# A decode block on one core: gate and up products moved behind the first scores, the down weights' load moved behind the fourth K tile

## The chip, the core and the metric

The kernel runs on one core of one Trainium2 chip. The metric is the device time of one execution in microseconds (us), the median of several runs. Its engines appear in the profile as PE (TensorE, matrix products; PEld is its weight load), DVE (VectorE), ACT (ScalarE), POOL (GpSimd) and SP (SyncE, which here only issues loads and the store of one output row). 16 DMA engines move the data; "SPq" is SP's issue queue.

## What is computed

One decode step for two sequences: attention over a cache of 32,768 keys with 32 query heads on 8 key/value heads, times the SiLU of a gated MLP, plus the input. All is float32.

```python
x = A_x                                   # [2, 1, 512]
xn = layernorm(x)
q = xn @ wq                               # 32 heads of 128
scores = q . k_cache * 128 ** -0.5        # k_cache [2, 8, 32768, 128]
s = (softmax(scores) @ v_cache) @ wo      # wo [4096, 512]
gate, up = xn @ W_gate, xn @ W_up         # [512, 1792] each
g = silu(((gate * (gate > 0)) * up) @ W_down)   # W_down [1792, 512]
return x + s * g
```

K and V caches together are 537 MB, which have to come from memory once; all weights are 28 MB.

## The kernel before

The work goes in 64 tiles. A tile is 8,192 keys of one sequence and one key/value head: four tiles make a group (one sequence, one head), 16 groups make all. A K tile is one load of 4 MB, [128 partitions, 4 chunks, 16 rows, 128]. V comes mostly in double tiles of 8 MB.

The loop of lines 524 to 567 runs over stages `s`. In stage `s`, DVE transposes K tile `s` in four parts (`k_transpose`, line 290, tile `kts`), with other DVE steps between the parts; PE makes the scores of tile `s` (`scores`, line 302, 32 matmuls); DVE copies the scores of tile `s - 1` out of PSUM (`take_scores`, line 316). Four stages later, after the softmax of the group (`tile_maximum`, `maximum`), come the tile's weights (`weights`, `take_weights`), and in odd stages the products of two tiles with V (`values`, line 374).

The small MLP is fitted into the first stages: `mlp_gu` makes the gate and the up product (32 matmuls each, line 242), `mlp_take` copies each out of PSUM (line 253), `mlp_h` gates them and transposes the result (lines 258 to 263), and `mlp_down` makes the down product (28 matmuls, line 277), whose SiLU is taken on ACT. The dictionaries `extra`, `taken` and `ahead` say in which stage such a step is called: `taken` right after `take_scores`, `extra` after the stage's scores and values, and `ahead` at the end of the stage, for loads.

What sets the order:

- PE and DVE run their instructions in the order of the calls: `pin` chains them, stage by stage. A step that waits holds all that is called later on its engine.
- All big loads go out through `load` (line 128) on SP's queue, in the order of the calls. SP waits in order too: a load whose buffer isn't free holds all loads behind it.
- The pool `ring` has two slots, tag "r". K tiles use them in turn, so K tile t + 2 can be loaded when the transposes of K tile t are done.
- The pool `wide` has one slot, tag "w". It holds one after the other `wq` (query weights), `wgu` (gate and up weights, two loads), `wd` (down weights), and then the double V tiles. Each of these loads waits until the last reader of the one before is done: `wd` for the up product, the first V tile for the down product.

The loads are called in this order before: wq, K0, K1, the two of wgu (before the loop); K2 (stage 0); wd, K3 (stage 1); K4 (stage 2); K5 and the first double V tile (stage 3); K6 (stage 4), and so on. In the text, K0 is the first K tile, K3 the fourth.

On PE the products of the MLP are called in this order: scores(0), scores(1), gate, up, scores(2), down, scores(3). `mlp_take` and `mlp_h` are called in stage 2, after `take_scores(1)`, and so stand on DVE between the first and the second part of K2's transposes.

Of the kernel before, what the change touches and what calls it, by code (L numbers as in the profile page):

```python
# [24 lines left out]
def kernel(  # L25
# [449 lines left out]
    extra, taken, ahead = {}, {}, {}  # L475

    def at(where, s, f, *a):
        where.setdefault(s, []).append((f, a))

    END = NK + NU  # L480
    at(ahead, 1, load_d)
    for s in range(NK - 2):
        at(ahead, s, load_k, s + 2)
        if s % 2 and s >= 3:
            at(ahead, s, load_vv, s - 3)
    at(ahead, NK - 2, load_v, NK - 4)
# [1 line left out]
    at(ahead, NK - 1, load_vv, NK - 2)  # L488
    at(ahead, NK + 1, load_wo, 0, 4)
    at(ahead, NK + 1, load_wo, 4, HKV)  # L490
    at(extra, 1, mlp_gu, "g")
    at(extra, 1, mlp_gu, "u")
    at(taken, 2, mlp_take, "g")
    at(taken, 2, mlp_take, "u")
    at(taken, 2, mlp_h)
# [107 lines left out]
```

## Time and profile before

| | us |
|---|---|
| median of 3 runs | 1330.86 |
| lowest, highest | 1330.72, 1330.94 |
| the profiled execution | 1330.93 |
| its span, first to last instruction | 1329.1 |

| engine | busy us | share of the span |
|---|---|---|
| PE (matmuls) | 908.2 | 68% |
| DVE | 707.1 | 53% |
| ACT | 52.1 | 4% |
| DMA queue of SP | | 98.6% of 16 engines |

How to read the lines that follow. A row of a timeline has the start in us, the duration in us, the engine, the line of the kernel, the operation, what it writes and reads with its shapes, and how many instructions were merged into the row; in brackets stands how long the engine was idle before and what ended that. A row of SP's issues (DMA_DIRECT2D) shows when a load was issued, not when it landed; merged rows reach from the first issue to the end of the last. A row of the waits has the waiting engine and line, what released it, the total in us, how often, and the longest. A row of a cut by time has the stretch, its length, the busy time and number of instructions of PE, PEld, DVE, ACT and POOL, then the clock granted to PE as a share of full speed, the mean busy share of the DMA engines, and the GB/s that they moved. The releaser of a wait is inferred by the profiler.

### The profile page before, as it was taken

Reading aid. Unit: us, or ns where it says so; the run is one execution under the profiler, and the core shown is the slowest. Engines: PE = TensorE matmul, PEld = TensorE weight load, DVE = VectorE, ACT = ScalarE, POOL = GpSimd, SP = SyncE. Lnnn points to the kernel's source line nnn. Section 1 sums busy time; section 2 is a strip of 40 time slices with the busy share of each in tenths; the row PEclk is TensorE's granted clock in tenths of the full one; section 3 lists DMA queues with packets and bytes.
Section 4 is the critical chain, followed back from the end, with each engine's and each line's share of the span. In section 5 each row is a group of like instructions: output and inputs, shape, how many; then the busy total and the mean of one; then the engine's idle time right before and its main releaser. Section 6 shows DMA issues by size and latency. Waiting matters only on the chain.

```text
span 1329.1 us, 10685 instructions
## 1 busy us (share of the span) xinstructions
PE 908.2 (68%) x4736; PEld 216.8 (16%) x4736; DVE 707.1 (53%) x667; ACT 52.1 (4%) x136; POOL 0.7 (0%) x6
## 2 busy tenths in 40 slices
PE   3586667776775776767568676757767676776775
PEld 1121111121111111111111111112111111111112
DVE  3848445466644546656454665545466554546610
ACT  0001000000000000000000000000000000000000
POOL 0000000000000000000000000000000000000000
PEclk9799788878878887878897778888889777987887
DMA  9979999999999999999999999999999999999997
GB/s 411 427 314 411 440 415 423 440 427 439 436 438 427 432 427 436 431 442 438 426 428 431 435 432 438 432 440 424 430 432 437 439 428 438 430 427 431 444 429 307
DMA packets 16962, 565.36 MB, mean 425 GB/s; under 512 B 1794, under 2 KB 1810, under 8 KB 3988
## 3 DMA queue, kind: packets, MB, share of 16 engines
q1 hardware_dynamic: 16888, 564.67, 98.6%
q8 instruction: 37, 0.61, 0.2%
q14 instruction: 9, 0.07, 0.0%
q10 hardware_dynamic: 28, 0.01, 0.0%
HBM read 564.67 MB, written 0.00 MB: 425 GB/s over the span
## 4 chain that ended last, share of the span: by engine, by line
DMA 66%; DVE 26%; PE 7%; issue 1%; DVEq 0%
DMA k<-in_A_k_cache_dram 60%; DVE kts L290 21%; DMA v<-in_A_v_cache_dram 5%; PE s L302 2%; PE o_ps L374 2%; DMA wq<-in_A_wq_dram 2%; DVE sc L316 1%; DVE os L396 1%; DVE ob L416 1%; PE pr L344 1%; PE pq L201 1%; DVE qt L220 0%; PE po L426 0%; PE py_near L446 0%; PE py L465 0%
## 5 line engine op out<-in xcount | busy, mean ns | idle before, releaser
L290 DVE STREAM_TRANSPOSE kts<-k 128x2048 f32<-128x2048 f32 x256 | 578.0, 2287 | 462.8 <-DMA k<-in_A_k_cache_dram 462.8
L302 PE MATMUL s<-kts,qt 128*32 128x512 f32 x2048 | 490.0, 729 | 186.6 <-DVE kts L290 183.3
L374 PE MATMUL o_ps<-v,sc 128*16 128x512 f32 x2048 | 258.7, 646 | 80.3 <-DMA v<-in_A_v_cache_dram 80.3
L302 PEld LDWEIGHTS s<-kts,qt 128*32 128x32 f32 x2048 | 97.0, 128 | 579.0 <-DVE kts L290 322.2
L374 PEld LDWEIGHTS o_ps<-v,sc 128*16 128x16 f32 x2048 | 62.4, 102 | 255.8 <-issue 167.1
L352 ACT ACTIVATE sc<-sc,nb 128x512 f32<-128x512 f32 x64 | 45.4, 710 | 1130.4 <-DVE nb L348 1130.4
L358 PE MATMUL pt<-sc,perm 128*128 128x512 f32 x128 | 85.4, 757 | 1.3 <-ACT sc L352 1.3
L316 DVE TENSOR_SCALAR_CACHE_REDUCE sc<-s 128x512 f32<-128x512 f32 x64 | 43.1, 673 | 58.9 <-PE s L302 58.9
L330 PE MATMUL pr<-ident,m 128*1 128x128 f32 x16 | 5.2, 327 | 79.3 <-DVE m L328 79.3
L367 DVE STREAM_TRANSPOSE sc<-pt 128x512 f32<-128x512 f32 x64 | 43.3, 676 | 12.7 <-PE pt L358 12.4
L344 PE MATMUL pr<-negone,mrow 1*128 1x1 f32 x32 | 8.9, 344 | 33.4 <-DVE mrow L341 33.4
L358 PEld LDWEIGHTS pt<-sc,perm 128*128 128x128 f32 x128 | 22.0, 215 | 54.1 <-issue 39.2
L413 PE MATMUL po<-os,head 128*4 128x512 f32 x32 | 28.2, 982 | 0.0
L394 DVE RECIPROCAL rl<-pl 128x1 f32<-128x1 f32 x16 | 2.6, 164 | 26.4 <-PE pl L389 26.4
L330 PEld LDWEIGHTS pr<-ident,m 128*1 128x1 f32 x16 | 1.3, 79 | 94.0 <-DVE m L328 92.1
L396 DVE SCALAR_TENSOR_TENSOR os<-o_ps,rl,own 128x512 f32<-128x512 f32 x16 | 12.0, 751 | 8.3 <-PE o_ps L374 6.8
L344 PEld LDWEIGHTS pr<-negone,mrow 1*128 1x128 f32 x32 | 7.5, 290 | 37.4 <-DVE mrow L341 37.4
L201 PE MATMUL pq<-wq,xt 128*32 128x512 f32 x64 | 8.8, 715 | 6.7 <-DMA wq<-in_A_wq_dram 6.7
L416 DVE TENSOR_REDUCE ob<-po 4x128 f32<-4x512 f32 x16 | 10.6, 662 | 4.5 <-PE po L413 4.3
L277 PE MATMUL ps_d<-wd,ht 128*32 128x512 f32 x28 | 12.2, 592 | 0.0
L352 ACT ACTIVATION_READ_ACCUMULATOR sc<-sc,nb 128x1 f32 x64 | 11.9, 186 | 0.0
L426 PE MATMUL po<-ident,ob 64*64 64x4 f32 x64 | 4.6, 244 | 10.5 <-DVE ob L416 10.5
(74 smaller groups left out, 107.6 us busy)
## 6 DMA issues: line engine op xcount, KB each, us to landing
k<-in_A_k_cache_dram SPq DMA_DIRECT2D x64, 4096.0 KB, 26.7
v<-in_A_v_cache_dram SPq DMA_DIRECT2D x2, 4096.0 KB, 29.5
wo<-in_A_wo_dram SPq DMA_DIRECT2D x7, 1024.0 KB, 17.7
wgu<-in_B_W_gate_dram SPq DMA_DIRECT2D x1, 3584.0 KB, 19.9
wgu<-in_B_W_up_dram SPq DMA_DIRECT2D x1, 3584.0 KB
wd<-in_B_W_down_dram SPq DMA_DIRECT2D x1, 3584.0 KB
wo<-in_A_wo_dram SPq DMA_DIRECT2D x1, 512.0 KB
wo<-in_A_wo_dram SPq DMA_DIRECT2D x2, 256.0 KB
```

The source lines that it names most:

```text
L201: nc.tensor.matmul(pq[half][32 * c : 32 * c + 32, :], xn[:, k, :], wqt[:, k, half, c * 512 : (c + 1) * 512], start=(k == 0), stop=(k == NK ...
L290: nc.vector.transpose(part.rearrange("p r e k -> p (r e k)"), KT[t][:, c].rearrange("p r d -> p (r d)"))
L302: nc.tensor.matmul(ps[Q * c : Q * c + Q, :], qt[:, b, hk, e, :], kts[c][:, :, e, :], start=(e == 0), stop=(e == 3),)
L316: nc.vector.tensor_scalar(ST[t].rearrange("p r m -> p (r m)"), SPS.pop(t), SCALE, None, op0=ALU.mult, op1=ALU.max, accum_out=MX[g][:, u : ...
L344: nc.tensor.matmul(pr[:, 256:257], mrow.rearrange("o c k h -> o (c k h)"), negone, start=True, stop=True)
L352: nc.scalar.activation(st, st, AF.Exp, bias=nbias, scale=1.0, accum_out=LS[g][:, u : u + 1])
L358: nc.tensor.matmul(PW[t], perm.rearrange("p k c h -> p (k c h)"), ST[t].rearrange("p r m -> p (r m)"), start=True, stop=True,)
L367: nc.vector.transpose(ST[t].rearrange("p r m -> p (r m)"), PW.pop(t))
L374: nc.tensor.matmul(ops[g % 2][a : a + NC * REP, :, :], w[:, r, : NC * REP], v[:, :, r, :], start=(u == 0 and r < 4), stop=(u == NU - 1 and ...
L396: nc.vector.scalar_tensor_tensor(OS[g], ops[g % 2], rl, own.unsqueeze(2).to_broadcast([P, NC, DH]), op0=ALU.mult, op1=ALU.mult,)
L413: nc.tensor.matmul(po[mine, :], head, o.rearrange("p c d -> p (c d)"), start=True, stop=True)
L416: nc.vector.reduce_sum(ob[mine, :], po[mine, :].rearrange("p (c d) -> p d c", c=NC), axis=AX.X)
```

## The change

The gate and up products are called in stage 0, behind scores(0), and no longer in stage 1, behind scores(1). The load of `wd` is called in stage 1 behind that of K3, and no longer ahead of it. The copies out of PSUM, the gating and the down product stay in stage 2, at their places. No instruction is added or taken away.

```diff
     END = NK + NU
-    at(ahead, 1, load_d)
     for s in range(NK - 2):
         at(ahead, s, load_k, s + 2)
+        if s == 1:
+            at(ahead, s, load_d)
         if s % 2 and s >= 3:
             at(ahead, s, load_vv, s - 3)
...
-    at(extra, 1, mlp_gu, "g")
-    at(extra, 1, mlp_gu, "u")
+    at(extra, 0, mlp_gu, "g")
+    at(extra, 0, mlp_gu, "u")
     at(taken, 2, mlp_take, "g")
     at(taken, 2, mlp_take, "u")
     at(taken, 2, mlp_h)
     at(extra, 2, mlp_down)
```

So the calls of the loads become wq, K0, K1, wgu, K2, K3, wd, K4, K5, first V tile, K6; and on PE scores(0), gate, up, scores(1), scores(2), down, scores(3).

## The prediction

> **What bounds the kernel now.** I read the page first: its busy shares, the DMA row over time, and the chain that ended last.
>
> ```profile
> span 1329.1 us, 10685 instructions
> DMA  9979999999999999999999999999999999999997
> GB/s 411 427 314 411 440 415 423 440 427 439 436 438 427 432 427 436 431 442 438 426 428 431 435 432 438 432 440 424 430 432 437 439 428 438 430 427 431 444 429 307
> DMA 66%; DVE 26%; PE 7%; issue 1%; DVEq 0%
> ```
>
> No engine is full, but the DMA engines are busy in nine tenths or more of nearly every slice, and two thirds of the chain is waiting for DMA. So the kernel lives on one stream of loads out of SP's queue. The exception is the third slice: 7 tenths and 314 GB/s. I cut that region by time, beside the long stretch after it.
>
> ```profile
> core 0: us, PE busy (x) PEld busy (x) DVE busy (x) ACT busy (x) POOL busy (x), PEclk, DMA share, GB/s
> 66.00:78.00 12.00, 9.79 (x92) 4.21 (x84) 5.63 (x8) 0.00 (x0) 0.00 (x0) 0.95 0.26 89
> 104.00:110.00 6.00, 4.58 (x28) 0.95 (x28) 4.60 (x3) 0.00 (x0) 0.00 (x0) 1.00 0.69 257
> 148.00:1300.00 1152.00, 800.20 (x4061) 185.07 (x4059) 621.72 (x540) 43.94 (x120) 0.00 (x0) 0.83 1.00 433
> 66.00:148.50 82.50, 60.06 (x319) 15.30 (x311) 43.28 (x36) 5.28 (x13) 0.00 (x0) 0.91 0.87 369
> 67.50:68.00 0.50, 0.50 (x12) 0.19 (x8) 0.00 (x0) 0.00 (x0) 0.00 (x0) 1.00 0.16 66
> 76.50:77.00 0.50, 0.00 (x0) 0.00 (x0) 0.48 (x1) 0.00 (x0) 0.00 (x0) 1.00 2.22 573
> ```
>
> The last column is GB/s. From 148 to 1300 us the stream moves 433 GB/s. From 66 to 78 us it moves 89 x 12 = 1.07 MB, which at 433 takes 2.5 us, so 9.5 us are lost: it all but stops before 67.5 us, I say at 67.3, and resumes between 76.5 and 77.0, I say at 76.7. From 104 to 110 us it moves 1.54 MB, worth 3.6 us: another 2.4 us lost. Together 11.9 us. The row from 66 to 148.5 checks it: 82.5 us at 369 GB/s is 30.4 MB, which at 433 is 70.3 us, so 12.2 us lost. I take 12.0.
>
> Who stops the stream? SP's own queue tells, its issues first, then what it waited for.
>
> ```profile
> 51.23 0.33 SPq L128 DMA_DIRECT2D k<-in_A_k_cache_dram  x1
> 75.82 0.33 SPq L128 DMA_DIRECT2D wd<-in_B_W_down_dram  x1
> 76.25 9.30 SPq L128 DMA_DIRECT2D k<-in_A_k_cache_dram  x2
> 106.08 0.33 SPq L128 DMA_DIRECT2D k<-in_A_k_cache_dram  x1
> 118.25 11.41 SPq L128 DMA_DIRECT2D k<-in_A_k_cache_dram  x2
> ...
> SPq L128 <- PE ps_u L242: 15.8, 1, 15.8
> SPq L128 <- DMA wgu<-in_B_W_up_dram: 8.4, 1, 8.4
> SPq L128 <- DVE sb_u L253: 0.2, 1, 0.2
> ```
>
> The issue at 51.23 is the third K tile (K2), the last thing in the stream when it dries up. Behind it in the queue stands wd (the down weights). It needs the one "w" buffer, which holds wgu until the gate and up products have read it: SP waits 8.4 us for the up weights to land (so they are there by 51.56 + 8.4 = 60.0 us), then 15.8 us for the last up product, and issues at 75.82. K3 stands behind wd and goes at 76.25. Was K3 held only by the queue? Its slot is K1's, which DVE gives free:
>
> ```profile
> 48.89 4.51 DVE L290 STREAM_TRANSPOSE kts<-k 128x2048 f32<-128x2048 f32 x2
> 58.37 6.69 DVE L290 STREAM_TRANSPOSE kts<-k 128x2048 f32<-128x2048 f32 x3
> 69.65 2.31 DVE L290 STREAM_TRANSPOSE kts<-k 128x2048 f32<-128x2048 f32 x1 [4.59 <-DMA k<-in_A_k_cache_dram]
> 71.88 0.65 DVE L316 TENSOR_SCALAR_CACHE_REDUCE sc<-s 128x512 f32<-128x512 f32 x1
> 75.83 0.62 DVE L253 COPY sb_u<-ps_u 128x448 f32<-128x448 f32 x1 [2.38 <-PE ps_u L242]
> 78.54 6.66 DVE L290 STREAM_TRANSPOSE kts<-k 128x2048 f32<-128x2048 f32 x3
> 96.54 2.31 DVE L290 STREAM_TRANSPOSE kts<-k 128x2048 f32<-128x2048 f32 x1 [11.34 <-DMA k<-in_A_k_cache_dram]
> 148.49 2.31 DVE L290 STREAM_TRANSPOSE kts<-k 128x2048 f32<-128x2048 f32 x1 [18.58 <-DMA k<-in_A_k_cache_dram]
> ```
>
> K1's four transposes end at 58.37 + 6.69 = 65.1 us. The same reading fits the other K issues: K2 goes at 51.23, when K0's last transpose is through, and the second issue in the 76.25 row (K4, 76.25 + 9.30 - 0.33 = 85.2) when K2's is, 78.54 + 6.66 = 85.2. So K3 was ready 11 us before it was issued, with 2 us of stream still ahead of it.
>
> **The change part by part.** No instruction and no byte is added or removed. Two things move.
>
> *wd behind K3 on SP.* K3's issue now follows K2's, and goes when K1's transposes are done: 65.1 us. From an issue to its first bytes is about 1.0 us (75.82 to the 76.5-77.0 window). The stream needs it by 67.3 - 1.0 = 66.3, so the gap closes with 1.2 us to spare. wd now waits in SP's queue with K4 behind it, and needs the gate and up products done.
>
> *The products behind scores(0).* The PE rows:
>
> ```profile
> 51.25 6.46 PE L302 MATMUL s<-kts,qt 128*32 128x512 f32 x28 [3.07 <-DVE kts L290]
> 65.11 4.23 PE L302 MATMUL s<-kts,qt 128*32 128x512 f32 x25 [0.28 <-DVE kts L290]
> 68.76 0.92 PE L242 MATMUL ps_g<-wgu,xt 128*32 128x448 f32 x6
> 75.25 0.54 PE L242 MATMUL ps_u<-wgu,xt 128*32 128x448 f32 x1
> 88.29 11.75 PE L277 MATMUL ps_d<-wd,ht 128*32 128x512 f32 x27
> 106.11 3.62 PE L302 MATMUL s<-kts,qt 128*32 128x512 f32 x26 [1.15 <-DVE kts L290]
> ```
>
> scores(0) ends at 57.7; PE then has little to do until K1's last transpose at 65.1. The 64 products took from 68.76 to 75.79, 7.0 us. Moved into that hole they run from 57.7 to 64.7 (the up half starts at 61.2, after its weights' 60.0). So wd can go at 65.5, right behind K3; the stream wants it by 76.0. scores(1) is not delayed: it still starts in earnest at 65.1. If the cover is gone (the products start only at 60.0 and run at half rate, 14 us), they end at 74.0, scores(1) waits behind them on PE, and DVE's take_scores(1) behind that; the price is worked out under the rivals.
>
> *What is late next.* I followed the queue with the stream as the clock: K tiles are 4,096 KB (4.19 MB, 9.7 us at 433), wd 3,584 KB (8.5 us), a double V tile twice a K tile, 19.4 us:
>
> ```profile
> k<-in_A_k_cache_dram SPq DMA_DIRECT2D x64, 4096.0 KB, 26.7
> wd<-in_B_W_down_dram SPq DMA_DIRECT2D x1, 3584.0 KB
> ```
>
> K2's bytes end at 67.3, K3's at 77.0, wd's at 85.5, K4's at 95.2, K5's at 104.9. Each issue is due 1.0 us before.
> - K4, due 84.5: K2 still lands at 69.65. After it DVE runs as before, but no longer waits for the up product: take_scores(1) at 71.88, the two product copies from 72.5, the second at about 73.1. From that copy to the end of K2's transposes was 85.20 - 75.83 = 9.4 us, so K4 goes at 82.5. Two us to spare.
> - K5, due 94.2: K3 is there, so DVE runs stage 3 straight on: one transpose to 84.7; scores(2) from 82.5 for 3.6 us (the 106.11 row) to 86.1; the copy 0.6; three transposes 6.7: 93.4. With scores(2) wholly at the slow rate (6.5 us, the 51.25 row) it is 96.3, and 2.1 us are lost. The row of the same work with PE freshly busy (65.11) has 4.2 us, and gives 94.0, in time. I take 0.3 us, between 0 and 2.1.
> - The first V tile, due 103.9: it needs the down product. wd's bytes end at 85.5 and land some 2.3 us later (K2: 67.3 to 69.65), so 87.8, about where the down product started before; it takes 12 us and ends at 99.9. In time. scores(3) now queues behind it on PE until 103.5, which delays DVE's stage 4, but K6 is due only at 104.9 + 19.4 - 1.0 = 123.3 and went 8.5 us after scores(3) (118.25 less 106.11 + 3.62), so 112 now. Cover: 11 us.
> - So the second gap (104 to 110), which came from K5 (106.08) waiting for K3's late transposes (the first at 96.54), also closes.
>
> From K6's landing on, everything waits for the stream: DVE stood idle 18.58 us before the 148.49 row. scores(3), with which its stage 4 starts, ends only 6 us earlier (103.5 against 106.11 + 3.62 = 109.7) while K6 lands 12 earlier, so some 12 us of this wait remain and nothing else becomes the bound. From there each landing simply moves up, to the tail. In the tail one thing hangs on when PE wakes:
>
> ```profile
> 1305.21 5.83 PE L374 MATMUL o_ps<-v,sc 128*16 128x512 f32 x32 [12.16 <-DMA v<-in_A_v_cache_dram]
> 1311.28 3.63 PE L374 MATMUL o_ps<-v,sc 128*16 128x512 f32 x32
> ```
>
> The same 32 products took 5.83 us after an idle stretch and 3.63 when running. Waking at another moment may cost up to 1.6 us more (all slow: 6.46 us for 28 at 51.25 makes 7.4 for 32) or 2.2 less; I take no difference.
>
> Sum: -12.0 + 0.3 = -11.7 us. The profiled execution took 1330.93 us, 1.8 beyond its span, and 0.07 more than the median of the runs shown; on the median, 1330.86 - 11.7 = 1319.2 us.
>
> **The rivals.** *K3 is held by something else* (the change doesn't do what it says). One row speaks for it: the 0.2 us wait that ends at 76.25 is put to the second product copy. If that is K3's true release, the copy's new time, 73.1, sets K3: bytes at 74.1 instead of 76.7, 2.6 us gained, and the second gap's 2.4, so 1325.9. Against it: that copy ends at 75.83 + 0.62 = 76.45, after the issue, and K2, K4 and K5 all went with a transpose. Chance 0.05.
>
> *PE is late.* Products ending at 74.0 as above. From their end to K4: scores(1)'s remainder 3.6, its copy 0.7, then 0.6 and 9.4 from the copies to the last transpose, 14.3 us. K4 at 88.3 against 84.5 loses 3.8: 12.0 - 3.8 = 8.2, so 1322.7. Against it: the clock column reads 0.50 at 56.5 and 1.00 at 57.0, just before the products start, and PE then stays busy.
>
> ```profile
> 56.50:57.00 0.50, 0.50 (x6) 0.06 (x2) 0.00 (x0) 0.00 (x0) 0.00 (x0) 0.50 0.40 172
> 57.00:57.50 0.50, 0.50 (x4) 0.00 (x0) 0.00 (x0) 0.00 (x0) 0.00 (x0) 1.00 1.73 745
> 60.50:61.00 0.50, 0.27 (x1) 0.18 (x2) 0.50 (x2) 0.00 (x0) 0.00 (x0) 0.50 1.97 852
> ```
>
> For it: the clock had fallen again at 60.5 after a 3 us pause. Chance 0.06.
>
> *Slower.* The same place, K4 behind wd behind the products, but with the products held on PE by their weights. Loss starts when they end after 84.5 - 14.3 = 70.2, eats the gain at 82.2 and passes 0.2% (2.7 us, about what a measurement can tell from no change) at 84.9: 1333.6 us and more. That needs the up weights to land 18 us later than 60.0 (84.9 less 7.0 is 77.9), and nothing ahead of them in the queue moves. Chance 0.03.
>
> *No change.* The stream, unbroken here, goes no faster than the 369 GB/s it averages with its gaps; then the gaps were no loss: 1330.9 us. Against it stands the 433 of the following 1152 us, with the same kinds of loads. [...] Chance 0.03.
>
> **How the numbers follow.** The forecast has 0.83. Its own range runs from -12.0 - 2.2 (nothing lost at K5, the tail all fast: 1316.7) to -12.0 + 2.1 + 1.6 (both at their worst: 1322.6). Both bounds of the tail at full length are unlikely, since it woke from idleness before and will again, so the low end is 1317.5; the high end reaches to PE being late, 1322.7. K3 held (0.05), no change and slower (0.03 each) stay outside. Faster by over 0.2%: 0.83 + 0.05 + 0.06 = 0.94; within 0.03; slower 0.03.
>
> **What would show it.** In the changed profile SP issues K3 at about 65 us and wd within 1 us of it; the windows from 66 to 78 and from 104 to 110 us read about 430 GB/s; the gate and up products run between 57.7 and 65; K4 goes near 82.5 and K5 near 93.5; DVE's wait before K6 ends at about 136.5 instead of 148.49, and lasts some 12 us instead of 18.6; from there the busy times per stage are as before. I am wrong if K3's issue comes with a copy rather than with a transpose, if a new hole opens ahead of K4, K5 or the first V tile, or if the 12 us gained at K6 are no longer there at the last V tile (1305.2 before, 1293 expected).

## The result, and the profile after

The changed kernel takes 1320.32 us (median of 5 runs, 1319.49 to 1322.04), the kernel before 1330.94 (5 runs): 10.6 us less, a ratio of 0.9922 (95% interval 0.9908 to 0.9935). The forecast was 1319.2, the range 1317.5 to 1322.7. The profiled execution is one of the longer ones: 1321.72 us, with a span of 1319.9, 9.2 less than the span before. Of the runs below, one execution (the first run of the early copies) took 1801.64 us, which nothing here explains; it is left out of that run's median and ratio.

The page of the changed kernel: span, DMA by slices, GB/s by slices.

```profile
span 1319.9 us, 10685 instructions
DMA  9999999999999999999999999999999999999997
GB/s 408 433 412 427 433 441 437 424 430 434 431 435 445 428 429 429 435 429 437 435 443 422 427 436 435 435 441 425 428 429 437 437 436 431 433 427 431 436 431 295
```

The third slice now reads 9 and 412; no slice but the last is below 408. Then the stream by stretches (last column GB/s, the clock granted to PE two columns before it):

```profile
66.00:78.00 12.00, 3.93 (x24) 0.63 (x13) 8.25 (x10) 0.00 (x0) 0.00 (x0) 0.78 1.00 429
78.00:84.00 6.00, 5.37 (x12) 0.76 (x16) 6.00 (x4) 0.00 (x0) 0.00 (x0) 0.50 0.96 416
90.00:96.00 6.00, 6.00 (x15) 1.54 (x14) 5.35 (x3) 0.00 (x0) 0.00 (x0) 1.00 0.90 388
96.00:104.00 8.00, 7.70 (x42) 1.94 (x40) 2.52 (x2) 2.35 (x5) 0.00 (x0) 1.00 0.95 373
104.00:110.00 6.00, 1.91 (x5) 1.08 (x5) 5.26 (x8) 1.93 (x5) 0.00 (x0) 0.74 1.20 519
148.00:1300.00 1152.00, 791.20 (x4086) 183.59 (x4085) 612.45 (x535) 43.93 (x120) 0.00 (x0) 0.83 1.00 433
```

66 to 78 us went from 89 to 429 GB/s, 104 to 110 from 257 to 519: both holes are gone. A shallow one has come in between: 388 and 373 from 90 to 104. SP's issues and the DVE rows show where:

```profile
52.31 12.98 SPq L128 DMA_DIRECT2D k<-in_A_k_cache_dram  x2
65.47 0.33 SPq L128 DMA_DIRECT2D wd<-in_B_W_down_dram  x1
82.42 13.28 SPq L128 DMA_DIRECT2D k<-in_A_k_cache_dram  x2
100.30 0.33 SPq L128 DMA_DIRECT2D v<-in_A_v_cache_dram  x1
...
69.68 2.31 DVE L290 STREAM_TRANSPOSE kts<-k 128x2048 f32<-128x2048 f32 x1 [4.74 <-DMA k<-in_A_k_cache_dram]
73.04 0.61 DVE L253 COPY sb_u<-ps_u 128x448 f32<-128x448 f32 x1
88.04 0.69 DVE L316 TENSOR_SCALAR_CACHE_REDUCE sc<-s 128x512 f32<-128x512 f32 x1 [3.45 <-PE s L302]
138.89 2.31 DVE L290 STREAM_TRANSPOSE kts<-k 128x2048 f32<-128x2048 f32 x1 [14.26 <-DMA k<-in_A_k_cache_dram]
```

K3 goes at 52.31 + 12.98 - 0.33 = 64.96 us (76.25 before), right when K1's transposes are done, wd at 65.47, K4 at 82.42, K5 at 82.42 + 13.28 - 0.33 = 95.37 (106.08 before), the first V tile at 100.30. K6 is there at 138.89 where it was at 148.49: 9.6 us of the 12.0 have arrived. Behind that the two executions are alike: the last V tile's products start at 1295.46 against 1305.21, 9.75 earlier, and the span is 9.2 shorter.

PE and its clock:

```profile
57.32 2.90 PE L242 MATMUL ps_g<-wgu,xt 128*32 128x448 f32 x25
60.36 2.87 PE L242 MATMUL ps_u<-wgu,xt 128*32 128x448 f32 x28
64.99 3.62 PE L302 MATMUL s<-kts,qt 128*32 128x512 f32 x26 [0.96 <-DVE kts L290]
80.26 1.91 PE L302 MATMUL s<-kts,qt 128*32 128x512 f32 x2 [0.28 <-DVE kts L290]
82.45 5.55 PE L302 MATMUL s<-kts,qt 128*32 128x512 f32 x26 [0.28 <-DVE kts L290]
88.09 11.75 PE L277 MATMUL ps_d<-wd,ht 128*32 128x512 f32 x27
...
85.50:86.00 0.50, 0.50 (x8) 0.13 (x4) 0.00 (x0) 0.00 (x0) 0.00 (x0) 0.50 0.61 262
86.50:87.00 0.50, 0.50 (x9) 0.13 (x2) 0.00 (x0) 0.00 (x0) 0.00 (x0) 1.00 0.15 66
```

The products stand in the hole behind scores(0) and are through before 64; scores(1) is on time. But scores(2) takes 5.55 us where 3.62 was counted: the clock column is at 0.50 until 86 us. Before the change the products ran up to 75.8; now PE has almost nothing to do from 68.6 to 78 (1.33 us of matmuls in 9.4). The clock falls at 72.73 and rises at 86.38: here it stayed at 0.50 through the two pairs of matmuls from 78 on, 1.91 us in every 2.2, and through the first 3.9 us of scores(2).

In other executions it rose earlier. Two experiments below run the same instructions up to scores(2), but for one that clears an added tile, and add work only later; in the profile of one of them (useless work in stage 9) the clock rises as the second pair ends, and scores(2) takes 3.62 us:

```profile
82.00:82.50 0.50, 0.46 (x1) 0.00 (x0) 0.50 (x1) 0.00 (x0) 0.00 (x0) 0.50 0.53 229
82.50:83.00 0.50, 0.26 (x4) 0.16 (x8) 0.50 (x2) 0.00 (x0) 0.00 (x0) 0.89 1.33 573
82.74 3.62 PE L310 MATMUL s<-kts,qt 128*32 128x512 f32 x26 [0.28 <-DVE kts L298]
```

In the clock records of the profiles before and after the change all changes of the clock lie whole multiples of 3.41 us apart (after it the fall at 72.73 and the rise at 86.38 are four such steps apart), and so do the two seen in stage 9's profile, a fall at 72.37 and a rise at 82.61, three steps. The steps don't lie at the same times in the three. After the change the step from 79.55 to 82.97 held 2.86 us of matmuls and the clock stayed at half; in stage 9's profile the step from 79.20 to 82.61 held 2.98 and it rose. What decides at the end of a step is not shown. What is measured is that the length of scores(2) differs between executions of one program: with the early copies of the experiments below it took 3.62 us in one profile and 4.67 in the other.

### The profile page after: what moved, and what is told of

Read it like the earlier page. It is cut to its first block, busy times and chain, and to the rows that moved or that the text cites. A ratio compares the mean times of both kernels' runs of the same rounds, so it can differ in the third digit from the quotient of the medians.

```text
span 1319.9 us, 10685 instructions
## 1 busy us (share of the span) xinstructions
PE 899.0 (68%) x4736; PEld 216.9 (16%) x4736; DVE 706.8 (54%) x667; ACT 52.1 (4%) x136; POOL 0.7 (0%) x6
## 4 chain that ended last, share of the span: by engine, by line
DMA 66%; DVE 26%; PE 7%; issue 1%; DVEq 0%
DMA k<-in_A_k_cache_dram 60%; DVE kts L290 21%; DMA v<-in_A_v_cache_dram 5%; PE o_ps L374 2%; DMA wq<-in_A_wq_dram 2%; PE s L302 2%; DVE sc L316 1%; PE ps_d L277 1%; DVE os L396 1%; DVE ob L416 1%; PE pq L201 1%; PE pr L344 1%; DVE qt L220 0%; PE po L426 0%; PE py L465 0%
## 5 line engine op out<-in xcount | busy, mean ns | idle before, releaser
L302 PE MATMUL s<-kts,qt 128*32 128x512 f32 x2048 | 482.7, 721 | 193.6 <-DVE kts L290 190.5
L374 PE MATMUL o_ps<-v,sc 128*16 128x512 f32 x2048 | 252.0, 635 | 77.6 <-DMA v<-in_A_v_cache_dram 77.6
L416 DVE TENSOR_REDUCE ob<-po 4x128 f32<-4x512 f32 x16 | 10.6, 662 | 4.5 <-PE po L413 4.3
L352 ACT ACTIVATION_READ_ACCUMULATOR sc<-sc,nb 128x1 f32 x64 | 11.9, 186 | 0.0
```

The source lines that it names most:

```text
L302: nc.tensor.matmul(ps[Q * c : Q * c + Q, :], qt[:, b, hk, e, :], kts[c][:, :, e, :], start=(e == 0), stop=(e == 3),)
L352: nc.scalar.activation(st, st, AF.Exp, bias=nbias, scale=1.0, accum_out=LS[g][:, u : u + 1])
L374: nc.tensor.matmul(ops[g % 2][a : a + NC * REP, :, :], w[:, r, : NC * REP], v[:, :, r, :], start=(u == 0 and r < 4), stop=(u == NU - 1 and ...
L416: nc.vector.reduce_sum(ob[mine, :], po[mine, :].rearrange("p (c d) -> p d c", c=NC), axis=AX.X)
```

## The experiments

Each ratio is to the kernel before on the run's own chip; the chips differ by some tenths of a us (the kernel before took 1330.94 to 1331.37 on them), so small differences between runs are read from the ratios. The theory is that of the prediction: what a run gains or loses is time in which the stream of loads is dry, and here it is dry ahead of K3 (before) or ahead of K5 (after). The rivals are that both parts of the change are needed, that the missing microsecond is lost in the tail, and that DVE work at this place costs its length whatever the stream does.

**Each part alone.** First only the queue order, with the products left in stage 1 (against the changed kernel):

```diff
-    at(extra, 0, mlp_gu, "g")
-    at(extra, 0, mlp_gu, "u")
+    at(extra, 1, mlp_gu, "g")
+    at(extra, 1, mlp_gu, "u")
```

> Only the queue order is changed: wd behind K3, the products stay in stage 1. Theory (the time is the holes in the stream, and each part alone closes the first): K3 goes at 65.1 us, wd at 75.8 just before it is due (76.0), K4 at 85.2 (0.7 late), K5 at about 95.8 (0.9 later still); so 1.6 of 12.0 us lost, time about 1320.5, as with both parts. Rival (both parts are needed, since wd without early products reopens the hole behind K3): wd late, K4 late behind it, no more than half of the gain, 1326 or more.

Measured: 1321.93 us (ratio to before 0.9927, 0.9915 to 0.9940). Then only the products, with wd ahead of K3 (against the kernel before):

```diff
-    at(extra, 1, mlp_gu, "g")
-    at(extra, 1, mlp_gu, "u")
+    at(extra, 0, mlp_gu, "g")
+    at(extra, 0, mlp_gu, "u")
```

> Only the products are moved to stage 0; wd stays ahead of K3. Theory (either part closes the first hole): wd goes at about 63.7 us, K3 at 65.1 behind it, no hole at 66 to 78; but K3 lands 8.5 us later than with both parts, so K5 goes at about 97 against 94.2 due: 3 us of the 12.0 lost, about 1322. Rival (the order in the queue is the cure, the products alone only shorten the wait): 1326 or more.

Measured: 1322.53 us (0.9934, 0.9921 to 0.9948). SP's issues and the stretches, of the queue order alone and then of the products alone:

```profile
51.25 14.13 SPq L128 DMA_DIRECT2D k<-in_A_k_cache_dram  x2
75.75 0.33 SPq L128 DMA_DIRECT2D wd<-in_B_W_down_dram  x1
85.15 11.35 SPq L128 DMA_DIRECT2D k<-in_A_k_cache_dram  x2
66.00:78.00 12.00, 9.72 (x92) 4.17 (x84) 5.65 (x8) 0.00 (x0) 0.00 (x0) 0.95 0.99 424
```

```profile
64.30 0.33 SPq L128 DMA_DIRECT2D wd<-in_B_W_down_dram  x1
65.63 32.13 SPq L128 DMA_DIRECT2D k<-in_A_k_cache_dram  x3
66.00:78.00 12.00, 5.16 (x28) 0.92 (x20) 8.26 (x10) 0.00 (x0) 0.00 (x0) 0.72 1.01 433
96.00:104.00 8.00, 5.36 (x36) 1.35 (x34) 6.56 (x6) 2.35 (x5) 0.00 (x0) 1.00 0.72 283
```

With the order alone K3 fills the stream until wd follows at 75.75; with the products alone wd goes at 64.30 and K3 right behind. Either way the stretch from 66 to 78 us is full (424, 433), so each part by itself closes the large hole; together they bring 0.0005 and 0.0012 of the time (0.7 and 1.6 us) over one alone, which the intervals don't separate. The price of the products alone is as computed: K3 comes behind wd, so K5 goes at 65.63 + 32.13 - 0.33 = 97.43, and from 96 to 104 us the stream has 283 GB/s, 2.8 us lost against 433. The rival that both are needed is out.

**The hole ahead of K5.** DVE waits 4.7 us for K2 at the end of stage 1 and has the MLP's copies and gating to do in stage 2, where they hold K4 and K5. So they are called earlier:

```diff
-    at(taken, 2, mlp_take, "g")
-    at(taken, 2, mlp_take, "u")
-    at(taken, 2, mlp_h)
+    at(extra, 1, mlp_take, "g")
+    at(extra, 1, mlp_take, "u")
+    at(extra, 1, mlp_h)
```

> The changed kernel, with the copies of the two products and the gating (3.3 us of DVE) called at the end of stage 1, where DVE waits 4.7 us for K2, and not between K2's transposes. Theory (what is missing of the 12 us is the hole ahead of K5): K4 goes at about 79, K5 at about 92, in time; the hole at 95 to 98 us closes and K6 lands 1.7 us or more earlier than in the changed kernel; time about 1318.5. Rival (the rest is lost in the tail, by the clock of PE): K5 earlier, but the time stays at 1320.3.

Measured: 1319.18 us (median of three; 0.9907, 0.9892 to 0.9922). The run was made again on one chip with the changed kernel:

> The changed kernel again, beside the one with the early copies, for a second profile. Theory: K6 lands 2 us later than with the early copies, time 1320.3.

> The kernel with the early copies again, on one chip with the changed kernel. Theory (hole ahead of K5 closed): 1 to 2 us less than the changed kernel, 1318.5 to 1319.3. Rival (the difference seen before was chance): the same as the changed kernel.

Measured: 1320.64 us for the changed kernel (0.9922, 0.9909 to 0.9936) and 1319.13 with the early copies (0.9909, 0.9895 to 0.9922), 1.5 us less. The intervals overlap; the rows of the profiles show the difference. SP's issue of K4 and K5, and the stretches, of the kernel with the early copies:

```profile
79.31 11.35 SPq L128 DMA_DIRECT2D k<-in_A_k_cache_dram  x2
136.62 2.31 DVE L290 STREAM_TRANSPOSE kts<-k 128x2048 f32<-128x2048 f32 x1 [9.82 <-DMA k<-in_A_k_cache_dram]
66.00:130.00 64.00, 45.16 (x171) 10.43 (x167) 41.34 (x32) 5.28 (x13) 0.00 (x0) 0.81 1.00 433
```

K5 goes at 90.33, the stream has its 433 GB/s all through, and K6 is there at 136.62, as forecast for the change (136.5). In the second profile of the changed kernel:

```profile
82.79 13.39 SPq L128 DMA_DIRECT2D k<-in_A_k_cache_dram  x2
139.93 2.31 DVE L290 STREAM_TRANSPOSE kts<-k 128x2048 f32<-128x2048 f32 x1 [14.86 <-DMA k<-in_A_k_cache_dram]
66.00:130.00 64.00, 46.47 (x181) 10.71 (x173) 43.08 (x35) 5.28 (x13) 0.00 (x0) 0.81 0.98 418
```

K5 at 95.85, 418 GB/s, K6 at 139.93. What the change left on the table is the hole ahead of K5, not the tail. The early copies make the kernel that beats both.

**The cost of a late K5.** Seven useless DVE transposes of 128x512 were put behind the first of K3's four transposes, ahead of the other three. They work on two added tiles, `junk` and `junk2`, and touch nothing that the output needs. (These lines stand above the loop, so line numbers in such a kernel are 8 higher.) In stage 3 of the changed kernel:

```diff
+    def idle_work(n):
+        for _ in range(n):
+            nc.vector.transpose(junk2, junk)
...
+    at(taken, 3, idle_work, 7)
```

> The changed kernel with 7 useless DVE transposes of 128x512 (some 0.6 us each, 4.2 us) put into stage 3 behind take_scores(2), ahead of the transposes that K5 waits for. Theory (K5 is already late, so each us more is a us of the stream): K5 at 99.6, K6 lands 4.2 us later, time 1324.5. Rival (the hole ahead of K5 costs nothing in the end, later slack takes it up): 1320.3.

Measured: 1324.42 us (0.9949, 0.9937 to 0.9962), 4.1 more than the changed kernel (3.6 by the ratios). K5 went at 98.68 and K6 was there at 141.21: 3.3 and 2.3 us later than in the changed kernel's profile, not 4.2, since scores(2) met the full clock in this execution (3.62 us) and so made up for part of the 5.2 us of useless work. The same in stage 9:

> The changed kernel with the 7 useless DVE transposes in stage 9, where the stream is unbroken and DVE waits for K tiles. Theory: no time, 1320.3. Rival (4 us of DVE cost 4 us anywhere): 1324.4.

Measured: 1321.44 us (0.9923, 0.9911 to 0.9936) beside 1320.64 for the changed kernel on that chip (0.9922): no difference that the intervals show, and less than the rival's 4 us. Behind the transposes of stage 9 DVE waits for the stream, 14.76 us in the changed kernel's profile (up to 216.27), and there the seven transposes, 5.2 us in stage 3, cost nothing that can be measured. And in stage 3 of the kernel with the early copies:

> The kernel with the early copies, with the same 7 useless DVE transposes in stage 3 that cost the changed kernel 4 us. There K5 went at 90.3 us, 3.9 us before it is due (94.2). Theory (only what is later than the stream's due time costs): K5 at about 94.4, nearly in time: at most 0.5 us over the kernel with the early copies, about 1319.5. Rival (DVE work at this place costs its length whatever the stream does): 1323.3.

Measured: 1322.51 us (0.9930, 0.9916 to 0.9943), 3.4 over the kernel with the early copies. The expectation missed. Its rows say why:

```profile
79.33 18.43 SPq L136 DMA_DIRECT2D k<-in_A_k_cache_dram  x2
85.64 5.18 DVE L130 STREAM_TRANSPOSE junk<-junk 128x512 f32<-128x512 f32 x7
79.35 5.64 PE L310 MATMUL s<-kts,qt 128*32 128x512 f32 x26 [0.28 <-DVE kts L298]
```

The seven transposes took 5.2 us, not 4.2, and scores(2) fell into the slow clock again (5.64 us against 3.62), so K5 went at 97.43, not at 94.4: 3.2 us behind the due time as I had it, and 3.4 us were paid. That fits the lateness better than the 5.2 us of work, but this run alone does not rule the rival out; the smaller doses below do.

**When K5 is due.** The stage 9 run had shown something else: there K5 went at 93.73, ahead of the 94.2 of the prediction, and K6 still came only at 138.85. So the useless work was made smaller, 2 and 4 transposes in the kernel with the early copies.

> The kernel with the early copies, with 2 of the useless DVE transposes in stage 3 (1.5 us by the 5.1 us that 7 took): K5 at 91.8 to 93.2 us. Theory as forecast (K5 is due at 94.2): no cost, K6 lands at 136.6, 1319.2. Rival (K5 is due earlier, between the 91.7 that cost nothing and the 93.7 that did): K6 up to 2 us later, up to 1321.

> The same with 4 useless transposes (3.0 us): K5 at 93.3 to 94.7. Theory as forecast (due at 94.2): K6 at 136.6 to 137.1, 1319.2 to 1319.7. Rival (due earlier): K6 at 138 to 139, 1320.5 to 1321.5, about the changed kernel's time.

Measured: 1318.74 us with 2 (0.9907, 0.9891 to 0.9924) and 1320.48 with 4 (0.9919, 0.9904 to 0.9934). SP's issue of K4 and K5 and the wait for K6, with 2 and then with 4:

```profile
79.50 12.69 SPq L136 DMA_DIRECT2D k<-in_A_k_cache_dram  x2
136.44 2.31 DVE L298 STREAM_TRANSPOSE kts<-k 128x2048 f32<-128x2048 f32 x1 [9.41 <-DMA k<-in_A_k_cache_dram]
```

```profile
79.46 14.84 SPq L136 DMA_DIRECT2D k<-in_A_k_cache_dram  x2
137.69 2.31 DVE L298 STREAM_TRANSPOSE kts<-k 128x2048 f32<-128x2048 f32 x1 [11.65 <-DMA k<-in_A_k_cache_dram]
```

K5 at 91.86 costs nothing, though it carries two of the transposes: the rival that DVE work here costs its length is out. At 93.97 it costs 1.1 us at K6, between what the two theories had forecast. The due time lies between 91.9 and 93.7, not at 94.2. It is not K4 that is late instead: its first transpose starts at 97.70 in the changed kernel and at 97.68 with the early copies, though K4 was issued at 82.42 and at 79.31. All profiled executions in the order of K5's issue (us):

| kernel | K5 issued | K6 there | time | time less K6 |
|---|---|---|---|---|
| early copies | 90.33 | 136.62 | 1318.74 | 1182.1 |
| early copies, again | 91.66 | 136.56 | 1318.78 | 1182.2 |
| early copies, 2 useless | 91.86 | 136.44 | 1318.67 | 1182.2 |
| changed, 7 useless in stage 9 | 93.73 | 138.85 | 1321.53 | 1182.7 |
| early copies, 4 useless | 93.97 | 137.69 | 1320.15 | 1182.5 |
| changed | 95.37 | 138.89 | 1321.72 | 1182.8 |
| changed, again | 95.85 | 139.93 | 1322.93 | 1183.0 |
| order alone | 96.17 | 139.63 | 1321.93 | 1182.3 |
| early copies, 7 useless | 97.43 | 139.71 | 1322.74 | 1183.0 |
| products alone | 97.43 | 139.76 | 1322.53 | 1182.8 |
| changed, 7 useless in stage 3 | 98.68 | 141.21 | 1324.42 | 1183.2 |
| before | 106.08 | 148.49 | 1330.93 | 1182.4 |

The last column moves by 1.1 us while the time moves by 12.3: what follows K6 is the same in all twelve to within that, and the time is decided by when K6 lands. K6 follows K5's issue only roughly: the issue at 93.73 cost more than that at 93.97.

## Why the prediction was right, and where it was off

- **The holes and their size.** Right. With no late K5 at all (early copies) K6 comes 11.9 to 12.1 us earlier than before; 12.0 had been taken from the GB/s of two stretches.
- **K3 and wd.** Right: 64.96 and 65.47 us against the 65.1 and 65.5 forecast. K3 goes with K1's last transpose; the rival that the product copy holds it is out (that copy starts at 73.04).
- **The products.** Right: they end before 64 us in the hole behind scores(0). PE was not late in that sense, and K4 went at 82.42 (82.5). But I listed as their cover only the time before K1's last transpose, and not that they had kept PE busy until 75.8 where they stood before. In the changed kernel the clock fell at 72.73 us, and scores(2) met the slow clock in both of its profiles (5.55 and 5.67 us), but not in the two with useless work only later (3.62 both). The prediction had the slow case as the bound "wholly at the slow rate" and took a case between; which of the two comes differed from profile to profile. That the products at their old place guard against it is not shown: before the change the clock also falls, at 80.90, and rises at 84.31, just ahead of scores(2) at 85.25.
- **K5.** This is the term that was mis-sized: 0.3 us taken, between 0 and 2.1. At K6 it cost 2.3 (138.89 against 136.5 to 136.6) in the first profile, which leaves about the 9.6 seen in that execution, and 3.4 in the second. Both lie beyond the bound. But both profiles show long executions of their runs (the second, at 1322.93, lies above the range itself), and the medians lost less: 10.6 us of the 12.0 arrived in the time. How much an execution loses hangs on how long scores(2) takes in it (3.62 to 5.67 us), so it is in part luck that the median came within 1.1 us of the forecast. Two things add up: K5 went 1.4 to 2 us later than the 93.4 to 94.0 worked out, where scores(2) met the slow clock, and it was due earlier than 94.2. In the run with the useless work in stage 9 scores(2) ran at the fast clock (K5 at 93.73), and K6 was as late as in the changed kernel, by the second alone; with 4 useless transposes (K5 at 93.97) the second cost only 1.1.
- **The lead of 1.0 us.** It was read from the stream's total, and that hides the 16 DMA engines. Counting the transfers under way in the traces shows them one by one (16 when all work). Before the change, after the issue of wd at 75.82, the first engine works at 76.8 but all 16 only at 77.8. The end of K4 is spread as well: in the changed kernel the first engine is idle at 95.4, only 3 still work at 96.2, and the last two begin with K5 at 99.0 and 99.5. From 66 to 130 us the stream has 433 GB/s in each of the three profiles with K5 out by 91.9, 425 in the run of stage 9 and 423 with 4 useless transposes; by these GB/s the two lose an estimated 1.2 and 1.5 us, and K6 came 2.3 and 1.1 later. The landing of K6 is spread too: in the changed kernel its 16 parts come in from 136.31 to 138.80, and DVE starts on it at 138.89, with the last. So the bytes missing in GB/s don't give what K6 loses. Why an engine takes up a load as late as 4.1 us after its issue (K5, 95.37 to 99.5) stays open.
- **The tail.** The bounds of -2.2 and +1.6 us for PE's waking were wider than what was seen: all that follows K6 differs by 1.1 us over the twelve profiles. From the last V tile's products to the end of the span it was 23.9 us before and 24.4 after, though those products took 5.83 and 4.92. In the profile of the early copies the last products wait, for 0.20 us, for the last of wo, so there the tail too ends with the stream:

```profile
1312.83 0.42 PE L465 MATMUL py<-wo,ots 128*32 128x128 f32 x8 [0.20 <-DMA wo<-in_A_wo_dram]
```

- **The rivals "slower" and "no change"** had nothing behind them: in the kernel with the early copies an unbroken stream moved 433 GB/s from 66 to 130 us, the same as it moved later on before the change.

## What to carry to other kernels

In a kernel that lives on one stream of loads, draw up a time table of the queue: when each load's bytes end, when the next must be issued, and which engine's instruction lets it go. Measure the time from an issue to the last DMA engine at work (4.1 us for K5 in the changed kernel), not to the first bytes (1.0), and allow for engines that run out one after the other (there from 95.4 us on, with 3 left at 96.2). No hole was made up for later here (what follows K6 took 1182.1 to 1183.2 us in all twelve profiles), and a hole can have several cures of which one is enough, as the large one had here; the next hole is set by the load with the least slack in that table, so give its work room there (here three DVE steps moved into a wait). Look at PE's clock behind the place that work is moved from, and count the burst there at its shortest and its longest (here 3.62 and 5.67 us), since its length differed between executions of one program (3.62 and 4.67).

## What the runs showed of the hardware

- Issuing a load 1.0 us before the stream runs dry wasn't enough here: with the bytes of K4 ending at about 95.2 us by the time table, an issue at 91.9 cost nothing, those at 93.7 and 94.0 cost 2.3 and 1.1 us. From an issue to all 16 DMA engines at work it took 2.0 us before the change (wd, 75.82 to 77.8) and 4.1 in the changed kernel (K5, 95.37 to 99.5).
- PE's clock stayed at half from 72.7 to 86.4 us in the changed kernel although from 78 on it had two pairs of slow matmuls, 1.91 us in every 2.2 us, and then scores(2). In the profile of the run of stage 9, with the same work up to there, it rose at 82.6. In the profiles before and after the change all changes of the clock lie whole multiples of 3.41 us apart; before it the clock falls at 80.90 and rises at 84.31, after it the times are 72.73 and 86.38.
